# Two masked slot outputs: from GpSimd to ScalarE, at the hand-over to the output phase

## The chip, the cores and the metric

The kernel runs on one core of one Trainium2 chip. The metric is the device time of one execution in microseconds (us). Where several executions are compared, their median is meant.

Engines are called as the profile calls them: PE is TensorE (PEld its weight load), DVE is VectorE, ACT is ScalarE, POOL is GpSimd, SP is SyncE, which issues most of the DMAs. A "q" behind an engine's name means its instruction queue.

## The reference

Two layers in a row. The first is a gated recurrence over time, and its output is at once the input of the second, a soft mixture of experts with slots.

```python
# first layer: x, f_logit are (4, 5056, 256), lower_bound is (256,)
f = lb + (1 - lb) * sigmoid(f_logit);  i = 1 - f
h[t] = f[t] * h[t-1] + i[t] * x[t]           # per batch row and channel; y = all h

# second layer: x = y as (20224, 256); phi (256, 32); w1 (8, 256, 1024); w2 (8, 1024, 256)
logits = x @ phi                             # 8 experts x 4 slots = 32 slots
d = softmax(logits, over tokens);   slot_input = d.T @ x
slot_out[e] = relu(slot_input[e] @ w1[e]) @ w2[e]
c = softmax(logits, over slots);    out = c @ slot_out      # (20224, 256) float32
```

## The kernel before

**First phase, to about 130 us.** Loops over units of a batch row and 512 tokens load `f_logit` and `x`, form the gate on ScalarE, transpose to channels on TensorE, scan on VectorE, transpose back, and form the exponentials of the logits. These stay in SBUF as `etall`: 128 partitions are 4 batch rows x 32 slots, the free dimension is time. The slot inputs are summed up in PSUM. From unit 9 on, expert weights are loaded through GpSimd's DMA queue (`load_w`, W_AT). The last weight, `w2_sb[E - 1]`, comes in three pieces, half, a quarter and a quarter (L144 to L147).

**Expert layers, about 131 to 143 us.** `hi` is the first product with ReLU; it is transposed (L643) into `hid` (experts 0 to 3) and `wide` (experts 4 to 7, L659). The column sums of the exponentials give `cs_ps` and their reciprocal `rcs`, one number for each partition (L653). The second product is summed up in the PSUM tile `so_ps`, whose 128 partitions are again 4 batch rows x 32 slots (L674). Its last matmuls run as the pieces of the last weight land, with small matmuls that nobody reads (`spin`, L152) in the gaps and behind the last.

**The hand-over, about 142.5 to 145 us.** This is the place of the change. VectorE makes `slot_out = so_ps * rcs` in bf16 (L692). GpSimd makes two masked copies `slot_bd[:, u] = slot_out * parity[:, u]` (L694): `parity` is 1 for the partitions of even batch rows in column 0 and for those of odd ones in column 1, so a product over 64 partitions gives two batch rows side by side (512 columns).

**Output phase, from 143 us.** A pool `pout` of eight PSUM buffers opens after the pools of the expert layers have closed. The order of the work is written out by hand in the last lines:

```python
whole(0, 0, ((0, 0, 1), (1, 1, 1), (0, 2, 2), (1, 4, 2), ...), (2, 4, 8, 12, 16))
couple(end, 0, (4, 7))
couple(end, 1)
whole(0, 1, [(t % 2, 2 * t, 2) for t in range(wide_r // 2)], (wide_r,))
rest()
...                       # then three couples of 16 rows
```

`whole` makes one batch row: its matmuls (L711) read `slot_out`, VectorE (L701) and ScalarE (L705) evict in turn, and SP stores after 2, 4, 8, 12 and 16 rows (L735). `couple` makes two batch rows with one matmul (L748) that reads `slot_bd`; VectorE evicts it with one instruction (L756) or ScalarE with two (L753); SP stores at L768 and L765. `rest` also reads `slot_bd`. The evictions multiply with `rrow`, the reciprocal row sums. The output buffers lie where the weights lay, so the first evictions wait for the weight DMAs too. Each engine runs its instructions in the order in which they are written (a manual schedule); waits between engines are put in by the framework, by tiles and by the release of pools.

Of the kernel before, what the change touches and what calls it, by code (L numbers as in the profile page):

```python
# [9 lines left out]
F32 = mybir.dt.float32  # L10
BF16 = mybir.dt.bfloat16
AX = mybir.AxisListType
ALU = mybir.AluOpType
ACT = mybir.ActivationFunctionType
# [4 lines left out]
def kernel(  # L19
# [10 lines left out]
    nc = tc.nc  # L30
    B, S, D = x.shape
    E = moe_w1.shape[0]
# [3 lines left out]
    P = 128  # L36
    DC = D // P
    FC = F // P
# [60 lines left out]
    parity = consts.tile([P, 2], F32, name="parity")  # L99
# [28 lines left out]
    slot_bd = store.tile([P, 2, D], BF16, name="slot_bd")  # L128
    slot_out = store.tile([P, D], BF16, name="slot_out")
# [3 lines left out]
    w2_sb = [wts.tile([P, FC, D], BF16, name=f"w2_sb{e}") for e in range(E - 2)]  # L133
# [16 lines left out]
    def spin(dst, k, w):  # L150
        for _ in range(k):
            nc.tensor.matmul(dst[:, ds(0, w)], w1_sb[0][:, 0, :P], w1_sb[0][:, 0, :w],  # L152
                             start=True, stop=True, skip_group_check=True)
# [8 lines left out]
    with tc.tile_pool(name="sp2", bufs=3) as sp2, \  # L162
# [223 lines left out]
        def row_sums(q0, q1):  # L386
            for i, (t0, n_r) in enumerate(blocks):
                ew = etall[:, ds(t0, P * n_r)].rearrange("s (p r) -> s p r", r=n_r)
                for r in range(n_r):
                    if q0 <= t0 // P + r < q1:  # L390
                        nc.tensor.matmul(sums[:, ds((t0 // P + r) * B, P)], ew[:, :, r], ones,
                                         start=True, stop=True, skip_group_check=True)
            if q1 == n_grp * R:
                nc.tensor.matmul(rs_ps[:, n_grp * R - 1, ds(0, B // 2)],
                                 left.rearrange("s t u -> s (t u)"), pair_ones,
                                 start=True, stop=True, skip_group_check=True)
# [207 lines left out]
    with tc.tile_pool(name="ew", bufs=1) as ew, \  # L604
         tc.tile_pool(name="pm", bufs=2, space=PSUM) as pm, \
         tc.tile_pool(name="pbig", bufs=1, space=PSUM) as pbig:

        rep2 = rep.rearrange("p b s -> p (b s)")

        sin = [ew.tile([P, NS], BF16, name=f"sin{o}") for o in range(DC)]  # L610
        nc.vector.tensor_scalar_mul(sin[0], sin_ps[:, 0], omlb[:, ds(0, 1)])
        nc.scalar.activation(sin[1], sin_ps[:, 1], ACT.Copy, scale=omlb[:, ds(1, 1)])

        cs1 = ew.tile([P, 1], F32, name="cs1")
        nc.vector.tensor_reduce(cs1, csum, AX.X, ALU.add)


        Q = 4
        H = F // 2
        his = []  # L620
        for q in range(E // Q):
            hi = ew.tile([P, F], BF16, name=f"hi{q}")
            for k in range(2):
                hi_ps = (psu.tile([P, H], F32, name="hi_ps", tag="up") if q == 0 else
                         pbig.tile([P, H], F32, name="hi_ps", tag=f"hi_ps{k}"))
                for o in range(DC):
                    for j in range(Q):
                        nc.tensor.matmul(hi_ps[ds(j * NS, NS)], sin[o],
                                         w1_sb[q * Q + j][:, o, ds(k * H, H)],
                                         start=(o == 0), stop=(o == DC - 1),  # L630
                                         skip_group_check=True)
                if k == 0:
                    nc.scalar.activation(hi[:, ds(k * H, H)], hi_ps, ACT.Relu)
                else:
                    nc.vector.tensor_scalar_max(hi[:, ds(k * H, H)], hi_ps, 0.0)
            his.append(hi)
        cs_ps = pm.tile([P, 1], F32, name="cs_ps", tag="pm")
        rcs = ew.tile([P, 1], F32, name="rcs")
        for q in range(E // Q):
            ht_ps = psu.tile([P, FC, P], BF16, name="ht_ps", tag="up")  # L640
            hi_v = his[q].rearrange("p (c f) -> p f c", f=FC)
            for fc in range(FC):
                nc.tensor.transpose(ht_ps[:, fc], hi_v[:, fc], ident)  # L643
            if q == 0:
                nc.tensor.matmul(cs_ps, rep2, cs1, start=True, stop=True)
                src = ht_ps.rearrange("p f (j s) -> p f j s", s=NS)[:, :, :, ds(0, SPE)]
                src = bass.AP(tensor=src.tensor, offset=src.offset,
                              ap=[list(src.ap[0]), [P, FC], [NS + SPE, Q], [1, SPE]])
                dst = hid[:, :, :, ds(0, SPE)]
                dst = bass.AP(tensor=dst.tensor, offset=dst.offset,  # L650
                              ap=[list(dst.ap[0]), [Q * NS, FC], [NS + SPE, Q], [1, SPE]])
                nc.scalar.copy(dst, src)
                nc.vector.reciprocal(rcs, cs_ps)  # L653
                continue
            for j in range(Q):
                s0 = (Q + j) * SPE
                src = ht_ps[:, :, ds(j * NS + s0, SPE)]
                copy = nc.scalar.copy if j % 2 == 0 else nc.vector.tensor_copy
                copy(wide[:, :, j, :, ds(s0, SPE)],  # L659
                     src.unsqueeze(2).broadcast_to([P, FC, B, SPE]))  # L660
        so4_ps = pm.tile([P, D], F32, name="so4_ps", tag="pm")
        for e in range(Q):
            for fc in range(FC):
                nc.tensor.matmul(so4_ps[ds(fc % 4 * NS, NS), :], hid[:, fc, e],
                                 w2_sb[e][:, fc],
                                 start=(e == 0 and fc < 4),
                                 stop=(e == Q - 1 and fc >= FC - 4),
                                 skip_group_check=True)
        so4 = ew.tile([P, D], F32, name="so4")
        nc.vector.tensor_copy(so4, so4_ps)  # L670
        so_ps = pm.tile([P, D], F32, name="so_ps", tag="pm")
        for j in range(Q):
            for fc in range(FC):
                nc.tensor.matmul(so_ps, wide[:, fc, j].rearrange("p b s -> p (b s)"),  # L674
                                 w2_sb[Q + j][:, fc], start=j == 0 and fc == 0,
                                 stop=j == Q - 1 and fc == FC - 1, skip_group_check=True)
                if j == Q - 1 and fc in (FC // 2 - 1, FC // 4 * 3 - 1):
                    spin(tail[:, 0], 5, NS)
            if j == 0:
                nc.tensor.matmul(so_ps, rep2, so4, start=False, stop=False,  # L680
                                 skip_group_check=True)
                row_sums(8, wide_r)
                nc.vector.reciprocal(rrow[:, :wide_r], rs_ps[:, :wide_r])
            if j == 1:
                row_sums(wide_r, n_grp * R)
                q = n_grp * R - 1
                nc.vector.reciprocal(rrow[:, wide_r:q], rs_ps[:, wide_r:q])
                nc.vector.reciprocal(rrow[:, q, ds(0, B // 2)], rs_ps[:, q, ds(0, B // 2)])
            if j == 2:
                spin(tail[:, 0], 6, NS)  # L690
        spin(tail[:, 0], 4, D)
        nc.vector.tensor_scalar_mul(slot_out, so_ps, rcs)  # L692
        for u in range(2):
            nc.gpsimd.tensor_scalar_mul(slot_bd[:, u], slot_out, parity[:, ds(u, 1)])  # L694


    held.close()
# [132 lines left out]
```

## Time and profile before

| | |
|---|---|
| median of 3 runs | 197.45 us (197.25 to 198.14) |
| profiled execution | 197.27 us, its span 195.5 us |
| busy share of the span | PE 78%, DVE 75%, ACT 70%, POOL 53% |
| DMA | 70.75 MB, of it 20.71 MB written; 362 GB/s on average |
| mean TensorE clock granted | 0.859 of full speed |
| last weights to first store (142 to 145 us) | DMA share 0.06, 0.02, 0.08 |
| DMA share from 145 to 193 us | 0.98 to 1.05 in the stages looked at |

The profile is one execution. "Idle before ... <-X" names what ended an engine's idle time; the chain is followed back from the last instruction to what released it. In the tables by window the columns are: window, length, busy time (and number) of PE, PEld, DVE, ACT, POOL, granted clock, DMA share, GB/s.

### The profile page before, as it was taken

The page shows a single profiled execution, that of the slowest core. Times are in us where ns is not written, and L with a number is a line of the kernel's source. Part 1 is how long each engine was busy: PE and PEld are TensorE (multiplying, and loading weights), DVE is VectorE, ACT ScalarE, POOL GpSimd, SP SyncE. Part 2 cuts the span into 40 slices and gives each one's busy share as a digit, 9 for nine tenths or more (in the row PEclk, how much of TensorE's full clock was granted, in tenths as well). Part 3 has the DMA queues.
Part 4 walks back from the last instruction along what each step waited for, and adds up shares of the span by engine and source line. Part 5 has one row for each costly group of instructions (what it writes and reads, how often), then busy time and mean ns, then how long its engine had stood idle before and what let it go on. Part 6 is the DMA issues. An engine that isn't in the chain of part 4 may idle for free.

```text
span 195.5 us, 3260 instructions
## 1 busy us (share of the span) xinstructions
PE 152.8 (78%) x1205; PEld 105.0 (54%) x1205; DVE 147.2 (75%) x188; ACT 137.3 (70%) x188; POOL 103.3 (53%) x78
## 2 busy tenths in 40 slices
PE   1687589977998979899797887989999999990000
PEld 1465448765685767668586675557974433220000
DVE  2669858999889999999999999814279897771000
ACT  3688674899998998989987597544069987682000
POOL 2589578575999779774969969392030000000000
PEclk9999958999999999999999999999995555555555
DMA  6999999999999999999999999999939999999995
GB/s 206 421 417 424 429 424 429 429 422 393 341 424 431 416 322 427 427 408 347 366 423 413 260 213 214 215 215 213 164 148 420 427 454 419 436 432 429 429 429 221
DMA packets 14145, 70.75 MB, mean 362 GB/s; under 512 B 1569, under 2 KB 2594, under 8 KB 10162
## 3 DMA queue, kind: packets, MB, share of 16 engines
q1 hardware_dynamic: 11504, 62.13, 76.8%
q0 software_dynamic: 2624, 8.42, 21.6%
q8 instruction: 9, 0.15, 0.3%
q14 instruction: 6, 0.05, 0.1%
q10 hardware_dynamic: 2, 0.00, 0.0%
HBM read 58.23 MB, written 20.71 MB: 404 GB/s over the span
## 4 chain that ended last, share of the span: by engine, by line
PE 37%; DVE 26%; ACT 11%; DMA 8%; issue 5%; POOL 2%; SPq 0%; ACTq 0%; DVEq 0%; POOLq 0%
DVE h L313 20%; PE op L748 10%; DMA f_t<-in_f_logit_dram 8%; DVE ht L343 5%; PE hp L326 4%; ACT oc L753 4%; PE sp L261 3%; ACT s_t L235 3%; PE up L267 3%; PE lg L357 2%; POOL u_t L246 2%; PE op L711 2%; PE slot_ps L183 2%; PE so_ps L674 2%; PE slot_ps L408 1%
## 5 line engine op out<-in xcount | busy, mean ns | idle before, releaser
L246 POOL TENSOR_TENSOR u_t<-s_t,x_t 128x1024 bf16<-128x1024 bf16 (+1 forms) x39 | 82.5, 2132 | 23.6 <-ACT s_t L235 10.4
L313 DVE TENSOR_TENSOR_SCAN h<-a,h,up 128x512 bf16<-128x512 f32 (+1 forms) x72 | 87.0, 1252 | 3.5 <-PE up L267 1.8
L235 ACT ACTIVATE s_t<-f_t 128x2048 bf16<-128x2048 f32 (+2 forms) x23 | 38.3, 1668 | 4.0 <-DMA f_t<-in_f_logit_dram 3.7
L326 PE MATMUL hp<-ident_f,h 128*128 128x128 f32 (+1 forms) x160 | 29.4, 308 | 7.9 <-DVE ht L343 6.8
L326 PEld LDWEIGHTS hp<-ident_f,h 128*128 128x128 f32 (+1 forms) x160 | 23.6, 207 | 18.1 <-DVE ht L343 12.4
L748 PE MATMUL op<-slot_bd,etall 64*128 64x512 bf16 x62 | 26.4, 581 | 1.0 <-ACT oc L753 0.3
L295 ACT ACTIVATE a<-sp,lbs 128x1024 f32<-128x1024 bf16 x24 | 25.4, 1112 | 1.3 <-PE sp L261 1.0
L261 PE MATMUL sp<-ident_f,s_t 128*128 128x128 f32 x144 | 21.0, 288 | 6.7 <-ACT s_t L235 4.2
L753 ACT ACTIVATE oc<-op,rrow 128x256 f32<-128x256 f32 x54 | 22.2, 489 | 5.0 <-PE op L748 4.8
L756 DVE TENSOR_TENSOR oc<-op,rrow 128x512 f32<-128x512 f32 x35 | 22.4, 685 | 3.4 <-PE op L748 3.3
L261 PEld LDWEIGHTS sp<-ident_f,s_t 128*128 128x128 f32 x144 | 16.9, 148 | 8.8 <-ACT s_t L235 5.1
L302 ACT ACTIVATE a<-sp,lbs 128x512 f32<-128x512 bf16 (+2 forms) x22 | 17.8, 857 | 3.8 <-PE sp L261 3.5
L267 PE MATMUL up<-ident_f,u_t 64*128 64x64 f32 x192 | 17.6, 229 | 2.1 <-POOL u_t L246 2.1
L183 PE MATMUL slot_ps<-rep,ident_f 128*128 128x256 f32 x54 | 18.2, 432 | 0.6 <-POOL rep L86 0.6
L748 PEld LDWEIGHTS <-etall 64*128 64x128 bf16 x62 | 8.9, 150 | 17.4 <-issue 13.1
L343 ACT COPY ht<-hp 128x512 f32<-128x512 f32 (+1 forms) x18 | 10.5, 583 | 10.2 <-PE hp L326 10.2
L267 PEld LDWEIGHTS up<-ident_f,u_t 64*128 64x128 f32 x192 | 13.9, 138 | 6.0 <-POOL u_t L246 2.5
L343 DVE COPY ht<-hp 128x512 f32<-128x512 f32 (+1 forms) x22 | 14.7, 668 | 2.4 <-PE hp L326 2.4
L705 ACT ACTIVATE ob<-op,rrow 128x256 f32<-128x256 f32 x15 | 6.0, 475 | 7.7 <-PE op L711 7.7
L313 DVE TENSOR_TENSOR_SCAN h<-a,up 128x512 bf16<-128x512 f32 x8 | 9.3, 1208 | 2.5 <-ACT a L302 1.7
L183 PEld LDWEIGHTS slot_ps<-rep,ident_f 128*128 128x128 f32 x54 | 8.8, 199 | 3.0 <-issue 1.1
L261 PE MATMUL up<-ident_f,u_t 128*128 128x128 f32 x48 | 9.5, 329 | 0.7 <-POOL u_t L246 0.6
(110 smaller groups left out, 148.3 us busy)
## 6 DMA issues: line engine op xcount, KB each, us to landing
f_t<-in_f_logit_dram SPq DMA_DIRECT2D x12, 1024.0 KB, 11.7
x_t<-in_x_dram SPq DMA_DIRECT2D x12, 1024.0 KB, 11.1
out_dram<-oc SPq DMA_DIRECT2D x6, 2048.0 KB, 13.1
w_sb<-in_moe_w_dram POOLq DMA_DIRECT2D x14, 512.0 KB, 9.7
f_t<-in_f_logit_dram SPq DMA_DIRECT2D x12, 512.0 KB, 8.5
x_t<-in_x_dram SPq DMA_DIRECT2D x12, 512.0 KB, 8.6
out_dram<-ob SPq DMA_DIRECT2D x1, 2048.0 KB, 10.4
out_dram<-oc SPq DMA_DIRECT2D x2, 896.0 KB, 6.9
```

Of the source, the lines that this page charges most:

```text
L183: nc.tensor.matmul(slot_bank[:, 1], ident_f, wide_rep, start=False, stop=False, skip_group_check=True)
L235: nc.scalar.activation(s_t, f_t, ACT.Sigmoid, scale=-1.0)
L246: nc.gpsimd.tensor_tensor(uts[n][:, :r], s_t[:, :r], x_t[:, :r], ALU.mult)
L261: nc.tensor.transpose(ps[:, :, r], t[:, r], ident_f)
L267: nc.tensor.transpose(v[:, :, r], t(r)[k].bitcast(F32), ident_f[k, k])
L295: nc.scalar.activation(a, sp[:, :, :, :, o], ACT.Identity, scale=nomlb[:, ds(o, 1)], bias=1.0)
L313: nc.vector.tensor_tensor_scan(h[:, :T, o], decays[n // 2, o][:, n % 2, :T], up[:, :T, o], hs[number(g - 1, b)][:, ds(used(g - 1) - 1, 1), ...
L326: nc.tensor.transpose(hp[:n_p, r], hw[:, :n_p, r], ident_f)
L343: copy(hts[g][:n_p, b].rearrange("p r d -> p (r d)").bitcast(F32), hps.pop(n)[:n_p].rearrange("p r c -> p (r c)"))
L748: nc.tensor.matmul(op.rearrange("p u d -> p (u d)"), ew[:, :, r], slot_bd[ds(j * 2 * NS, 2 * NS)].rearrange("s u d -> s (u d)"), start=Tru ...
L753: nc.scalar.activation(ob[:, u, r], op[:, u], ACT.Copy, scale=scale[:, r, ds(u, 1)])
L756: nc.vector.tensor_tensor(ob[:, :, r], op, scale[:, r].unsqueeze(2).broadcast_to([P, 2, D]), ALU.mult)
```

## The change

GpSimd's two products of `slot_out` and `parity` go. In their place GpSimd makes, early, `half_rcs = parity * rcs` (two columns), and ScalarE makes both halves of `slot_bd` straight from `so_ps`, scaled by a column of `half_rcs`. GpSimd's last instruction is now a copy of one column of the last weight piece into a new tile, `landed`, which nobody reads. Everything else, the order of the matmuls, evictions and stores included, is the same.

```diff
@@ -636,6 +636,7 @@
         cs_ps = pm.tile([P, 1], F32, name="cs_ps", tag="pm")
         rcs = ew.tile([P, 1], F32, name="rcs")
+        half_rcs = ew.tile([P, 2], F32, name="half_rcs")
@@ -651,6 +652,7 @@
                 nc.scalar.copy(dst, src)
                 nc.vector.reciprocal(rcs, cs_ps)
+                nc.gpsimd.tensor_scalar_mul(half_rcs, parity, rcs)
                 continue
@@ -691,7 +693,9 @@
         spin(tail[:, 0], 4, D)
         nc.vector.tensor_scalar_mul(slot_out, so_ps, rcs)
         for u in range(2):
-            nc.gpsimd.tensor_scalar_mul(slot_bd[:, u], slot_out, parity[:, ds(u, 1)])
+            nc.scalar.activation(slot_bd[:, u], so_ps, ACT.Copy, scale=half_rcs[:, ds(u, 1)])
+        landed = ew.tile([P, 1], BF16, name="landed")
+        nc.gpsimd.tensor_copy(landed, w2_sb[E - 1][:, FC - 1, ds(0, 1)])
```

## The prediction

> **What bounds the kernel now.** I read the slices of the page first, then the chain in order of time, then stages by window, then single rows around the edit.
>
> The edit stands in the hand-over from the expert layers to the output phase. The chain in order of time shows what carries that hand-over:
>
> ```profile
> 142.45 0.03 issue
> 142.47 0.49 DVE slot_out L692
> 142.97 0.05 issue
> 143.02 0.45 PE op L711 x2
> ...
> 143.54 2.69 ACT ob L705 x7
> ```
>
> (Columns: start, length, what.) The last matmul of `so_ps` ends at 142.45; VectorE scales it into `slot_out`; the first output matmuls of L711 follow within 0.07 us; the evictions follow those. GpSimd's two instructions of L694, which make `slot_bd`, are not in this chain. The stages say why the end hangs on it:
>
> ```profile
> 142.00:143.00 1.00, 0.87 (x12) 0.54 (x10) 0.48 (x1) 0.00 (x0) 0.00 (x0) 1.00 0.06 16
> 143.00:144.00 1.00, 0.98 (x9) 0.99 (x10) 0.56 (x2) 0.46 (x2) 0.86 (x1) 1.00 0.02 8
> 144.00:145.00 1.00, 0.98 (x9) 0.83 (x8) 1.00 (x3) 1.00 (x4) 0.97 (x2) 1.00 0.08 25
> 145.00:146.00 1.00, 0.97 (x5) 0.65 (x6) 1.00 (x3) 1.00 (x4) 0.00 (x0) 1.00 1.05 404
> 146.00:150.00 4.00, 3.70 (x14) 1.40 (x13) 4.00 (x8) 4.00 (x12) 0.00 (x0) 0.65 1.04 422
> 160.00:170.00 10.00, 9.63 (x22) 2.90 (x20) 7.93 (x13) 7.78 (x20) 0.00 (x0) 0.50 1.01 426
> 180.00:190.00 10.00, 0.00 (x0) 0.00 (x0) 0.00 (x0) 0.00 (x0) 0.00 (x0) 0.50 1.04 444
> 193.00:195.50 2.50, 0.00 (x0) 0.00 (x0) 0.00 (x0) 0.00 (x0) 0.00 (x0) 0.50 0.03 13
> ```
>
> The last two columns are the DMA share and GB/s. From 142 to 145 the DMA engines are almost empty: the weights have landed and nothing is ready to store. From 145 to 193 they are full, and for the last 16 us no engine works at all. So the end is the moment of the first store plus 20.71 MB at some 430 GB/s. Is the stream ever short of work? The nearest point is 161.3, where the first of the big `couple` stores is issued: by then 8.13 MB have been issued (2.10 + 1.84 + 1.84 + 2.10 + 0.26 from the shapes) and about 6.95 MB moved (the windows added up), a cover of 1.2 MB or 2.7 us. So a delay of the first store moves the end by the same amount, and work later than the first stores is free up to about 2.7 us.
>
> The rows of the edit, with two lines from 135 us that matter below:
>
> ```profile
> 135.06 0.27 ACT L659 COPY wide<-ht_ps 128x128 bf16<-128x128 bf16 x1 [0.59 <-PE ht_ps L643]
> 135.36 0.23 DVE L659 COPY wide<-ht_ps 128x128 bf16<-128x128 bf16 x1 [0.79 <-ACT wide L659]
> 135.62 0.27 ACT L659 COPY wide<-ht_ps 128x128 bf16<-128x128 bf16 x1 [0.29 <-DVE wide L659]
> ...
> 142.47 0.48 DVE L692 TENSOR_SCALAR slot_out<-so_ps,rcs 128x256 bf16<-128x256 f32 x1 [1.54 <-PE so_ps L674]
> ...
> 143.14 1.84 POOL L694 TENSOR_SCALAR slot_bd<-slot_out,parity 128x256 bf16<-128x256 bf16 x2 [9.64 <-DVE slot_out L692]
> 143.54 2.69 ACT L705 ACTIVATE ob<-op,rrow 128x256 f32<-128x256 f32 x7 [7.66 <-PE op L711]
> 144.09 3.10 SPq L735 DMA_DIRECT2D out_dram<-ob  x5
> 145.03 1.68 PE L748 MATMUL op<-slot_bd,etall 64*128 64x512 bf16 x8
> ```
>
> `slot_bd` is ready at 144.98 and its first reader, L748, starts at 145.03; but TensorE is busy with the sixteen matmuls of L711 until 144.99 anyway. ScalarE stands idle for 7.66 us up to 143.54, GpSimd for 9.64 us up to 143.14.
>
> **The change part by part.**
>
> *GpSimd's pair of L694 goes* (2 x 923 ns). It is wholly beside TensorE's L711; the gap it can have caused is the 0.04 us between 144.99 and 145.03, ahead of stores that have over 2 us of cover. Gain: 0.
>
> *`half_rcs` on GpSimd* (a 128x2 product) is queued behind the `left` copies, which end at 133.49, and waits for `rcs` (134.57). The nearest row, a 32x64 copy, takes 255 ns. Done by about 135, 8 us ahead of its reader; nothing but `landed` is queued behind it. Cost 0; uncovered it would cost its 0.26.
>
> *`landed` on GpSimd* waits for the last weight DMA. The matmul that reads that piece started at 142.06, so it has landed by then; GpSimd answered VectorE 0.19 us after the end of `slot_out` (142.95 to 143.14), and 0.26 us as above makes it done by some 142.6. In the built instruction stream the first evictions of VectorE and ScalarE now also wait for GpSimd's count that `landed` raises. Before, they started at 143.44 and 143.54, so 0.8 us are in hand: cost 0.
>
> *Two ScalarE instructions, `so_ps` to `slot_bd`.* If they ran beside `slot_out` in ScalarE's idle 7.66 us, they would be nearly free. They don't. In the built stream the first waits for VectorE's count after `slot_out` (and GpSimd's for `half_rcs`), not for TensorE's: both engines read one PSUM tile and are put one after the other, as the three L659 rows above show two readers of `ht_ps` being made to take turns. And the first matmul of L711, until now released by `slot_out`, waits in addition for ScalarE's count after the second: the pool `pout` takes over PSUM once `so_ps` is released. TensorE is in order, so all 16 matmuls, the evictions and every store queued on SP stand behind that wait. The pair goes onto the path:
> - ScalarE's answer to VectorE: 0.03 us (135.59 to 135.62 in L659) to 0.09 (134.12 to 134.21, TensorE to ScalarE at L652, which has semaphore instructions ahead as here). I take 0.09.
> - the pair: same form, PSUM to 128x256 with a column as scale, is L705 at 475 ns and in overlapped pairs 0.83 to 0.86 us; bf16 instead of f32 output changes little (128x512: 598 against 583 ns). I take 0.85; with no overlap it is 2 x 0.489 = 0.98 (L753's mean).
> - TensorE's answer to ScalarE: 0.00 (135.89, L674 after `wide`) to 0.06 (126.56 to 126.62, L442). I take 0.03.
> - what it replaces, `slot_out`'s end to the first matmul: -0.07.
> - the first weights are loaded during the wait: up to -0.10 (a weight load of L711 is 142 ns, partly hidden already); and one more semaphore instruction ahead of the first evictions, about 0.05 (a row of those: 49 ns), at most 0.10. I let the two cancel.
>
> The Trainium skill, ScalarE: Activation LUTs, What ACT_TABLE_LOAD costs, gives an activation 186 ns plus 0.833 ns per element plus 93 ns for a pointer operand, with 93 ns of overlap back to back; an estimate from it is 0.89 us for the pair, and the sum would be 0.94. The trace's pairs are 0.85, so its durations stay.
>
> Sum: 0.09 + 0.85 + 0.03 - 0.07 = **+0.90 us**; all low ends 0.03 + 0.83 + 0.00 - 0.07 - 0.10 = 0.69, all high ends 0.09 + 0.98 + 0.06 - 0.07 + 0.10 = 1.16. `slot_out` ends at 142.95 as before, the first matmul moves from 143.02 to 143.92, the first store from 144.09 to about 145.0. What is late next is the whole store stream. The extra ScalarE work is then done in time in which ScalarE would wait for L711 anyway.
>
> The profiled execution took 197.27 us (195.5 of span and 1.77 around it), 0.18 below the median of 197.45. It becomes 198.17; on the median, **198.35**, or 0.46% more. About 0.5%, or 0.99 us, is what a measurement of this kernel can tell from no change, so the forecast is slower, but near that line.
>
> **Rivals.**
>
> *Absorbed* (not slower, about 197.45). The delay reaches the first store and is won back by slack in the stream, since in 160 to 180 the engines move 426 and 421 GB/s against 444 in 180 to 190: 20 us at 5% less is 1.0 us. For: just this difference. Against: the share is still 0.98 to 1.01 there, and whatever paces that stretch starts from the same late hand-over. It decides if the compute after 150 catches up, which the cover at 161.3 says it need not. A smaller form is that the pair starts with `slot_out`: 142.47 + 0.05 + 0.85 + 0.03 = 143.40, so +0.38. The Trainium skill, PSUM — Partial Sum Buffer, PSUM bank collisions raise a hardware error, has it that two engines, two readers too, must be kept apart by semaphores within one bank; by that rule this form is out, and the trace agrees with the L659 rows (ScalarE 0.29 us idle for VectorE).
>
> *Faster.* GpSimd held back more than its row shows: without its 1.84 us beside VectorE's evictions these run quicker and the stream fills sooner. Against: VectorE's 128x512 evictions take 0.68 us beside GpSimd and 0.68 in L756 without it. To win 1 us net it would have to give 1.9. No row pays that.
>
> *Slower by more.* `landed` is late: both first evictions stand behind GpSimd, whose reaction to a DMA's landing no row gives. It decides when `landed` ends after 144.3 (first matmul at 143.92 plus 0.42 to its eviction), that is 1.7 us later than I put it; a microsecond beyond that gives 0.90 + 0.5 to 1.0, some 199.1. Unmeasured costs of alternating two readers on one bank would land here too.
>
> *The change does not do what it says* is closed: the built stream has the two activations, GpSimd's pair is gone.
>
> **How the numbers follow.** The serial pair: 0.72. Its bounds 0.69 to 1.16 hold the line of 0.99 at about two thirds, and the scatter of single runs (197.25 to 198.14) blurs it, so I split it 0.32 above the line, 0.40 within. Absorbed or overlapped: 0.07, within. Faster: 0.06. More than the pair: 0.15, above the line. That is slower 0.47, same 0.47, faster 0.06. The range takes the pair (198.14 to 198.61), the absorbed case down to 197.4, and most of the larger delays, up to 199.0; outside remain the faster case and the late end of the last one.
>
> **What would show it.** Right: ScalarE's two `slot_bd` rows start at about 143.04, not at 142.5, with VectorE's `slot_out` as releaser; the first L711 matmul of the new kernel (a few lines further down in the file) near 143.9, released by ScalarE; the first store near 145.0; the windows of 143 to 145 both under 0.1 DMA share; full from 146 to 194; span about 196.4. Wrong in the sum: the pair longer than 0.98, or `landed` ending after 144. Wrong in kind: a first store still at 144.1; or a late first store with an unchanged end, which would mean that the stream had slack.

## The result, and the profile after

The changed kernel takes 198.47 us (median of 22 runs) against 197.45 before (22 runs): the ratio is 1.0053, 95% interval 1.0039 to 1.0066, or +1.05 us (0.77 to 1.30). The profiled execution took 198.51 us with a span of 196.7; before it was 197.27 with 195.5.

The timeline of the changed kernel around the hand-over (start, length, engine, line, operation; its lines are two to four further down in the file than before):

```profile
142.22 0.19 POOL L698 COPY landed<-w_t 128x1 bf16<-128x1 bf16 x1 [7.66 <-DMA w_t<-in_moe_w_dram]
...
142.63 0.48 DVE L694 TENSOR_SCALAR slot_out<-so_ps,rcs 128x256 bf16<-128x256 f32 x1 [2.16 <-PE so_ps L676]
...
143.23 0.84 ACT L696 ACTIVATE slot_bd<-so_ps,half_rcs 128x256 bf16<-128x256 f32 x2 [7.81 <-DVE slot_out L694]
144.12 1.90 PE L715 MATMUL op<-slot_out,etall 32*128 32x256 bf16 x16 [1.09 <-ACT slot_bd L696]
...
144.47 2.81 DVE L705 TENSOR_TENSOR ob<-op,rrow 128x256 f32<-128x256 f32 x5 [1.36 <-PE op L715]
144.65 2.66 ACT L709 ACTIVATE ob<-op,rrow 128x256 f32<-128x256 f32 x7 [0.59 <-ACT slot_bd L696]
145.15 3.03 SPq L739 DMA_DIRECT2D out_dram<-ob  x5
```

ScalarE's pair is released by VectorE's `slot_out`, though its data, `so_ps`, were complete before `slot_out` began; and TensorE's first output matmul is released by ScalarE's pair, though its own operand, `slot_out`, had been ready for a microsecond. The windows show that the empty stretch of the DMA engines has become a slice longer, and that the stream ends more than a microsecond later:

```profile
143.00:144.00 1.00, 0.02 (x1) 0.14 (x1) 0.11 (x1) 0.77 (x2) 0.00 (x0) 1.00 0.03 8
144.00:145.00 1.00, 0.88 (x9) 0.88 (x9) 0.53 (x2) 0.41 (x2) 0.00 (x0) 1.00 0.06 16
145.00:146.00 1.00, 1.00 (x11) 0.84 (x10) 1.00 (x2) 1.00 (x4) 0.00 (x0) 1.00 0.03 8
...
193.00:195.50 2.50, 0.00 (x0) 0.00 (x0) 0.00 (x0) 0.00 (x0) 0.00 (x0) 0.50 0.52 223
```

Before, the slice from 145 had a DMA share of 1.05; here it has 0.03. The last row had 13 GB/s before and has 223 here: half of those 2.5 us are still stores.

One thing is needed to read the rest. Executions of every kernel here, the one before included, scatter by 0.7 us and more, and their profiles reach `slot_out` at moments between 142.40 and 143.82, with a hand-over that doesn't depend on it. So a profile is read from the end of its own `slot_out` (before 142.95, after 143.11), and times are compared by ratios over many runs.

### The profile page after: what moved, and what is told of

It is laid out like the page before. It is cut to its first block, busy times and chain, and to the rows that moved or that the text cites. A ratio compares the mean times of both kernels' runs of the same rounds, so it can differ in the third digit from the quotient of the medians.

```text
span 196.7 us, 3265 instructions
## 1 busy us (share of the span) xinstructions
PE 153.8 (78%) x1205; PEld 106.0 (54%) x1205; DVE 147.1 (75%) x188; ACT 138.1 (70%) x190; POOL 101.6 (52%) x78
## 5 line engine op out<-in xcount | busy, mean ns | idle before, releaser
L752 PE MATMUL op<-slot_bd,etall 64*128 64x512 bf16 x62 | 27.0, 608 | 0.7
L261 PE MATMUL sp<-ident_f,s_t 128*128 128x128 f32 x144 | 22.0, 298 | 6.1 <-ACT s_t L235 4.3
L261 PEld LDWEIGHTS sp<-ident_f,s_t 128*128 128x128 f32 x144 | 17.7, 153 | 8.0 <-ACT s_t L235 5.1
L183 PE MATMUL slot_ps<-rep,ident_f 128*128 128x256 f32 x54 | 17.7, 423 | 0.0
L357 PE MATMUL lg<-h,phi 128*32 128x512 bf16 (+1 forms) x80 | 9.6, 389 | 0.0
```

The source lines that it names most:

```text
L183: nc.tensor.matmul(slot_bank[:, 1], ident_f, wide_rep, start=False, stop=False, skip_group_check=True)
L261: nc.tensor.transpose(ps[:, :, r], t[:, r], ident_f)
L752: nc.tensor.matmul(op.rearrange("p u d -> p (u d)"), ew[:, :, r], slot_bd[ds(j * 2 * NS, 2 * NS)].rearrange("s u d -> s (u d)"), start=Tru ...
```

## The experiments

Theory S: ScalarE's pair stands between `slot_out` and the first output matmul, the first store is late by that, and the end is late by the same. In the table the second column is the first matmul and the third the first store, both after the end of `slot_out` in that kernel's profile. The fourth is the third minus the 1.14 of before. The last is the ratio of the times, minus 1, times 197.5; the ratio is to runs of the kernel before that were made beside them (median 197.72 us beside x1 to x4, 197.46 beside x5 to x8).

| kernel | matmul | store | store, against before | time, against before (95%) |
|---|---|---|---|---|
| before | 0.07 | 1.14 | 0 | 0 |
| x1: small GpSimd instructions alone | 0.06 | 1.16 | +0.02 | -0.20 (-0.55 to +0.16) |
| x5: GpSimd's pair twice | 0.06 | 1.12 | -0.02 | +0.12 (-0.26 to +0.51) |
| x2: ScalarE from `slot_out` | 0.05 | 1.36 | +0.22 | +0.36 (-0.06 to +0.77) |
| x6: VectorE's pair | 0.06 | 1.57 | +0.43 | +0.38 (+0.06 to +0.69) |
| x3: one ScalarE instruction | 0.65 | 1.70 | +0.56 | +0.57 (+0.26 to +0.91) |
| x7: change without `landed` | 1.01 | 1.97 | +0.83 | +0.87 (+0.40 to +1.34) |
| the change | 1.01 | 2.04 | +0.90 | +1.05 (+0.77 to +1.30) |
| x4: four ScalarE instructions | 1.74 | 3.06 | +1.92 | +1.80 (+1.22 to +2.37) |
| x8: first store of one row | 0.06 | 1.04 | -0.10 | +0.47 (+0.14 to +0.81) |

Down to x4 the two last columns agree within the intervals. That is the main result. The profiles say the same more sharply: from the first store to the end of the span it is 51.4 us before (195.5 - 144.09), and 51.4 too in x1, x2, x3, x4, x6 and x7, whether the first store is late by nothing or by 1.92. It is 51.6 in the change, 51.8 in x5 and 52.2 in x8; these three are taken up below.

**x1, the small GpSimd instructions alone.**

```diff
+        half_rcs = ew.tile([P, 2], F32, name="half_rcs")
+                nc.gpsimd.tensor_scalar_mul(half_rcs, parity, rcs)
+        landed = ew.tile([P, 1], BF16, name="landed")
+        nc.gpsimd.tensor_copy(landed, w2_sb[E - 1][:, FC - 1, ds(0, 1)])
         nc.vector.tensor_scalar_mul(slot_out, so_ps, rcs)
```

> The kernel before, with the two small GpSimd instructions of the change added (half_rcs after rcs, landed ahead of slot_out) and GpSimd still making slot_bd; both new tiles are read by nobody. Theory S (the whole loss is ScalarE's pair standing between slot_out and the first output matmul): the first L711 matmul follows slot_out's end by 0.07 us as before, the time is that of before within 0.1 us. Rival U (the 0.15 us or so of the loss that the hand-over doesn't explain, 1.05 measured against 0.90 from slot_out's end to the first store, comes from GpSimd's extra instructions or the waits on landed): 0.1 to 0.2 us slower than before.

Measured 197.50 us, ratio 0.9990 (0.9972 to 1.0008). S holds. U is out at 0.2 us; a cost of 0.1 is still inside the interval.

**x7, the change without `landed`.**

```diff
-        landed = ew.tile([P, 1], BF16, name="landed")
-        nc.gpsimd.tensor_copy(landed, w2_sb[E - 1][:, FC - 1, ds(0, 1)])
```

> The changed kernel without landed; GpSimd's last instruction is half_rcs. Theory S: landed ended 0.7 us before slot_out's end in the changed kernel's profile (142.41 against 143.11), so nothing waited for it: the time stays at +1.0 us over before, within 0.15 us of the change. Rival L (part of the loss is the wait of the first evictions on landed): 0.1 to 0.3 us faster than the change.

Measured 198.47 us, the same median as the change; ratio to before 1.0044 (1.0020 to 1.0068). The first matmul is 1.01 us after `slot_out` here too, so the main part of the loss is not `landed`'s. The times, +0.87 and +1.05 with intervals of 0.3 to 0.5 us to either side, can't tell L's 0.1 to 0.3 us from nothing. The profiles put `landed` at 0.07 us: ScalarE's first eviction follows the first matmul after 0.46 us here and after 0.53 in the change, and the first store comes 1.97 instead of 2.04 us after `slot_out`.

**x2, ScalarE from `slot_out`.**

```diff
-            nc.gpsimd.tensor_scalar_mul(slot_bd[:, u], slot_out, parity[:, ds(u, 1)])
+            nc.scalar.activation(slot_bd[:, u], slot_out, ACT.Copy, scale=parity[:, ds(u, 1)])
```

> The kernel before, with ScalarE making slot_bd from slot_out in SBUF (scaled by parity) in place of GpSimd; so_ps has VectorE as its only reader, no half_rcs, no landed. Theory S: the first output matmul is back at 0.07 us after slot_out's end; ScalarE's pair runs from 143.05 to 143.9, beside the first matmuls, so ScalarE's first eviction starts at about 143.95 in place of 143.54 and the first store 0.4 us later than before; time 0.4 us over before (197.85). Rival R (the loss is what ScalarE's two added instructions cost wherever they stand): as slow as the change, +1.05. Rival A (the store stream has slack): no change.

Measured 197.98 us, ratio 1.0018 (0.9997 to 1.0039): +0.36 us, and R's +1.05 is out. The timeline of x2 shows the same two ScalarE instructions, about as long as in the change (0.91 us against 0.84), beside the matmuls instead of ahead of them:

```profile
143.82 0.49 DVE L692 TENSOR_SCALAR slot_out<-so_ps,rcs 128x256 bf16<-128x256 f32 x1 [1.53 <-PE so_ps L674]
144.34 0.91 ACT L694 ACTIVATE slot_bd<-slot_out,parity 128x256 bf16<-128x256 bf16 x2 [7.10 <-DVE slot_out L692]
144.36 1.96 PE L711 MATMUL op<-slot_out,etall 32*128 32x256 bf16 x16
```

So most of the loss isn't ScalarE's work itself, but what waits for it. With `so_ps` no longer read by ScalarE, TensorE no longer waits for ScalarE. What is left, 0.22 us at the first store, is ScalarE's first eviction behind its pair, and smaller than the 0.4 expected.

**x3, one ScalarE instruction.**

```diff
-        for u in range(2):
-            nc.scalar.activation(slot_bd[:, u], so_ps, ACT.Copy, scale=half_rcs[:, ds(u, 1)])
+        nc.scalar.activation(slot_bd[:, 0], so_ps, ACT.Copy, scale=half_rcs[:, ds(0, 1)])
+        nc.gpsimd.tensor_scalar_mul(slot_bd[:, 1], slot_out, parity[:, ds(1, 1)])
```

> The changed kernel with one ScalarE instruction from so_ps (half 0) instead of two; half 1 is made by GpSimd from slot_out as before, with no landed. Theory S: the first output matmul waits for 0.47 us of ScalarE instead of 0.84, so it follows slot_out's end by about 0.64 us against 1.01 in the changed kernel and 0.07 before; time 0.55 to 0.6 us over before. Rival R (a fixed price of putting a second reader on the PSUM tile, not the length of its work): about as slow as the change, +0.9 to 1.05.

The expectation is wrong in one word: the kernel that ran does hold `landed`, behind GpSimd's half. Measured 198.25 us, ratio 1.0029 (1.0013 to 1.0046): +0.57 us, as S says. R's 0.9 lies at the very end of the interval (0.91); the first store, late by 0.56 and not by 0.90, speaks against it. The timeline of x3 shows something besides:

```profile
143.58 0.47 ACT L695 ACTIVATE slot_bd<-so_ps,half_rcs 128x256 bf16<-128x256 f32 x1 [7.17 <-DVE slot_out L694]
144.11 1.90 PE L715 MATMUL op<-slot_out,etall 32*128 32x256 bf16 x16 [0.73 <-ACT slot_bd L695]
144.44 0.18 POOL L698 COPY landed<-w_t 128x1 bf16<-128x1 bf16 x1
144.66 2.81 DVE L705 TENSOR_TENSOR ob<-op,rrow 128x256 f32<-128x256 f32 x5 [1.20 <-POOL landed L698]
144.66 2.67 ACT L709 ACTIVATE ob<-op,rrow 128x256 f32<-128x256 f32 x7 [0.60 <-POOL landed L698]
```

The matmul is 0.65 us after `slot_out` (0.64 expected). But `landed` ends at 144.62, behind GpSimd's half, and both first evictions are named as released by it: VectorE's starts 0.55 us after the matmul where the change has 0.35, ScalarE's 0.55 where it has 0.53. This is the prediction's third rival, a late `landed`, brought about by an order on GpSimd's queue that the change doesn't have. It costs next to nothing here, since the first store waits for ScalarE's eviction too, which ends later: the store follows the matmul by 1.05 us, in the change by 1.03. In the change it ended at 142.41, before `slot_out` began.

**x4, four ScalarE instructions.**

```diff
-        for u in range(2):
+        for u in (0, 1, 0, 1):
             nc.scalar.activation(slot_bd[:, u], so_ps, ACT.Copy, scale=half_rcs[:, ds(u, 1)])
```

> The changed kernel with ScalarE's pair made twice (the second pair writes the same values again). Theory S: the first output matmul follows slot_out's end by 1.9 us (0.84 to 0.9 more than in the change) and the time is 1.85 to 2.0 us over before, one for one with the delay of the first store. Rival A (the stream wins part of a delay back): the first store as late, but the time well under 1.7 us over before.

Measured 199.35 us, ratio 1.0091 (1.0062 to 1.0120): +1.80 us. The timeline of x4:

```profile
143.00 1.57 ACT L696 ACTIVATE slot_bd<-so_ps,half_rcs 128x256 bf16<-128x256 f32 x4 [7.19 <-DVE slot_out L694]
144.62 1.90 PE L715 MATMUL op<-slot_out,etall 32*128 32x256 bf16 x16 [1.82 <-ACT slot_bd L696]
```

All four overlapped, so the matmul is 1.74 us after `slot_out` and not 1.9. ScalarE's first eviction came 0.82 us after the matmul instead of 0.53; the profile doesn't say why. At the first store this is +1.92, and the time follows. A, a stream that wins part back, is out above some 0.7 us (1.92 against the lower bound of 1.22); the profile shows nothing won back, since the span ends 51.4 us after the first store, as before.

**x5, GpSimd's pair twice.**

```diff
-        for u in range(2):
+        for u in (0, 1, 0, 1):
             nc.gpsimd.tensor_scalar_mul(slot_bd[:, u], slot_out, parity[:, ds(u, 1)])
```

> The kernel before with GpSimd's pair made twice (same values written again), so that slot_bd is ready 1.8 us later, near 146.9 instead of 144.98 in the profile of before. Theory S (only the first store's moment counts; work behind the first stores has cover): L748 starts 1.8 us later, the first store stays at 1.14 us after slot_out's end, and the time stays within 0.3 us of before, since 2 MB of stores issued by 147.2 keep the DMA engines busy to about 149.9 and the next store of before was issued at 148.1. Rival E (every delay of the hand-over shows at the end, whichever engine makes it): +1.8 us.

Measured 197.74 us, ratio 1.0006 (0.9987 to 1.0026). The timeline of x5:

```profile
143.94 3.63 POOL L694 TENSOR_SCALAR slot_bd<-slot_out,parity 128x256 bf16<-128x256 bf16 x4 [10.50 <-DVE slot_out L692]
...
147.62 2.94 PE L748 MATMUL op<-slot_bd,etall 64*128 64x512 bf16 x9 [1.84 <-POOL slot_bd L694]
```

TensorE now really stands still for GpSimd, for 1.84 us, and the kernel is slower by at most 0.5 us. E is out. But the cover isn't quite enough. The first store comes no later than before, yet the span ends 51.8 us after it, 0.4 more than before, and the windows of x5 show a stream that is short of work for a while, where the kernel before has DMA shares of 1.02 and 1.01:

```profile
150.00:151.00 1.00, 0.93 (x5) 0.22 (x2) 1.00 (x3) 0.98 (x3) 0.00 (x0) 0.50 0.81 332
151.00:152.00 1.00, 1.00 (x3) 0.28 (x2) 1.00 (x3) 1.00 (x4) 0.00 (x0) 0.50 0.76 311
```

So in this execution some 1.4 of the 1.84 us were covered, an estimate from 1.84 less 0.4. The same `slot_bd` costs half a microsecond at most when it is 1.8 us later on GpSimd, because only L748 waits for it, and a whole one when ScalarE makes it early, because L711 waits for ScalarE's reading of `so_ps`.

**x6, VectorE's pair.**

```diff
-            nc.gpsimd.tensor_scalar_mul(slot_bd[:, u], slot_out, parity[:, ds(u, 1)])
+            nc.vector.tensor_scalar_mul(slot_bd[:, u], slot_out, parity[:, ds(u, 1)])
```

> The kernel before with VectorE making slot_bd from slot_out in SBUF, in the 0.49 us in which it waits for the first output matmul. Theory S: the first matmul stays at 0.07 us after slot_out's end; the pair costs between 0.3 and 0.55 us (the nearest rows: 224 ns for a 128x128 bf16 copy, 251 ns for a 128x32 product, both from PSUM), so VectorE's first eviction moves by at most 0.1 and the first store by 0 to 0.1 us: the time is that of before within 0.2 us. Rival R (an added instruction between slot_out and the evictions always costs its length): +0.4 us or more.

Measured 197.91 us, ratio 1.0019 (1.0003 to 1.0035): +0.38, a miss, and by its number nearer to rival R's +0.4. The timeline of x6:

```profile
143.93 0.48 DVE L694 TENSOR_SCALAR slot_bd<-slot_out,parity 128x256 bf16<-128x256 bf16 x2
143.95 1.96 PE L711 MATMUL op<-slot_out,etall 32*128 32x256 bf16 x16
...
144.90 2.81 DVE L701 TENSOR_TENSOR ob<-op,rrow 128x256 f32<-128x256 f32 x5 [0.49 <-PE op L711]
```

The pair is as long as expected (0.48) and TensorE isn't delayed, but VectorE's first eviction starts 0.95 us after the first matmul, not 0.42, and 0.49 us after the pair. Ahead of that eviction stand six semaphore instructions, all of them waits for DMAs (shortest, median and longest in ns, then the first and the last start; the kernel before, then x6):

```profile
L701 DVEq EVENT_SEMAPHORE  x6: 49/50/50, 142.5 to 143.3; - x6
L701 DVEq EVENT_SEMAPHORE  x6: 49/50/50, 143.9 to 144.8; - x6
```

In the kernel before three of them run during `slot_out` and three between 143.15 and 143.40, when VectorE has nothing else to do. In x6 one runs beside the pair; the other five follow each other behind it, one every 0.10 us, from 144.41 to 144.86, and the eviction starts 0.04 us later. They fill the 0.49 us. A kernel without them wasn't run, so that they are the whole cause is read from the trace and not tried. R's "always" doesn't hold all the same: in x2 the 0.91 us of ScalarE cost 0.22 at the first store.

**x8, a first store of one row.**

```diff
-                     (0, 10, 2), (1, 12, 2), (0, 14, 2)), (2, 4, 8, 12, 16))
+                     (0, 10, 2), (1, 12, 2), (0, 14, 2)), (1, 2, 4, 8, 12, 16))
```

> The kernel before with the first store after one row instead of two (one store more; SP stores after 1, 2, 4, 8, 12 and 16 rows). Theory S: the first store waits for VectorE's first row alone (143.86 in the profile of before, against 144.01 for ScalarE's), so it is issued 0.13 us earlier and the time is 0.1 to 0.15 us below before, at the edge of what five rounds can tell. Rival: the smaller store leaves a gap behind it, or costs as much as it gains: no change or up to 0.1 us slower.

Measured 198.02 us, ratio 1.0024 (1.0007 to 1.0041): +0.47, a miss in sign. The first store is 0.10 us earlier, as meant, but the span ends 52.2 us after it, 0.8 more than before. The windows of x8 show a part of that as a hole behind the first store:

```profile
144.00:145.00 1.00, 0.96 (x10) 0.84 (x9) 1.00 (x3) 1.00 (x4) 0.90 (x1) 1.00 0.20 73
145.00:146.00 1.00, 1.00 (x4) 0.49 (x4) 1.00 (x2) 1.00 (x4) 0.00 (x0) 0.65 0.72 256
```

Before, the two slices held shares of 0.08 and 1.05, together 1.13; here 0.20 and 0.72, together 0.92. SP needs 3.33 us for its six issues instead of 3.10 for five; that the larger stores come too late behind two small ones would fit the hole, but wasn't tried by itself.

The other part lies at the very end, behind the stores. When the last store has landed, SP still has to run what is left of its closing semaphore instructions (L825; SP has twelve there in both kernels). Before, one is left ahead of the final drain, 28 ns at 194.6 us; in x8 eight are left, from 194.9 to 195.3. From the last landing to the end of the span it is 0.90 us before and 1.32 in x8. These 0.42 us of the profile are nearly the +0.47 measured. That the added store put the closing waits into another order is likely, but wasn't tried. So x8 doesn't test the moment of the first store by itself. None of these kernels was shown to be faster than the kernel before.

## Why the prediction was right

**The place.** The two waits that it read from the built stream are the releasers that the trace names: VectorE's `slot_out` for ScalarE, ScalarE's `slot_bd` for TensorE.

**The size.** ScalarE answered in 0.12 us (0.09 taken), the pair took 0.84 (0.85 taken), TensorE answered in 0.05 (0.03 taken), less the 0.07 of before: 0.94 at the first matmul, 0.04 more than forecast. ScalarE's first eviction, which ends later than VectorE's and so releases the first store, follows the matmul after 0.53 us instead of 0.52. Without `landed` (x7) it is 0.46, so the two small terms that were set against each other come out at -0.06 and +0.07, and do cancel. SP answers that eviction 0.04 us sooner than before, which the prediction didn't name, and the first store follows the matmul after 1.03 instead of 1.07. That makes 0.90 at the first store, the number forecast; that it fits to the hundredth is luck. The estimate that was worked out from the Trainium skill, ScalarE: Activation LUTs, What ACT_TABLE_LOAD costs, 0.89 us for the pair, lies 0.05 above the row; a single one has 470 ns in the trace against its 492.

**One for one.** The step from the first store to the end rested on a full DMA stream and on 2.7 us of cover for later work. x4 (+1.92 and +1.80, and 51.4 us from the first store to the end) bears out the first. The cover was put too high. The prediction took 161.3 us for the nearest point at which the stream could run short; 148.1, where the first `couple` store is issued, is nearer. Counted in the same way, 2.10 MB had been issued and some 1.3 MB moved by then, a cover of 0.8 MB or 1.8 us, and x5 with its 1.84 us lost about 0.4. The forecast doesn't hang on it: in the change that store follows the first one by 4.0 us, as before. The absorbed case is gone with x4. Its smaller form, the pair beside `slot_out`, is gone by the releaser in the timeline, which also agrees with the rule of the Trainium skill, PSUM — Partial Sum Buffer, PSUM bank collisions raise a hardware error, that two readers of one bank are kept apart. No run here lets both read at once.

**The free parts.** `half_rcs` took 0.29 us and ended at 134.55; `landed` 0.19, ended at 142.41. x1 and x7 show no cost of either in the times; at the first store `landed` costs the 0.07 us named above.

**What is left.** The time rose by 1.05 us, 0.15 more than the store. The two profiles, 1.24 us apart, differ in two places besides: by 0.16 ahead of `slot_out` (142.63 against 142.47), where the kernels are alike but for `half_rcs`, and by 0.17 behind the first store (51.58 us to the end of the span against 51.41). x1 shows no cost of the first kind. x7, the change without `landed`, has nothing of the second and measures +0.87. The interval of the time reaches from 0.77, so the rest is most likely scatter; it wasn't settled. With 0.53% the change stands just above the line of 0.5%, on which the forecast put its chances evenly.

## What to carry to other kernels

When work is moved from a slow engine off the path to a fast one, ask who will wait for it there, not how long it takes: here 1.84 us of GpSimd were free, and 0.84 us of ScalarE cost all of their length, because here the second reader of a PSUM tile waited for the first, and the first matmul of the next pool waited for both. Where a full DMA stream sets the end, measure an edit ahead of it by the moment from which the stream runs without a gap, and look at what stands behind the last store as well (x8). And look at what waits ahead of an engine's first instruction of a new phase, since work placed there can uncover it.

## What the runs showed that had not been expected

An instruction put into VectorE's idle 0.49 us (x6) fitted in length, 0.48 us, and still moved the first eviction by 0.53 us. A store that was issued 0.10 us earlier (x8) came with a kernel 0.47 us slower, and 0.42 us of its profile lie behind the last landing, in closing waits. And 1.84 us of standing still (x5) used up a cover that had been put at 2.7.
